# A table of offsets to a planner's priorities, and new planned durations, in a one-core attention and MLP kernel

## The chip, the cores and the metric

The kernel runs on one core of a Trainium2 chip. The metric is the device time of one execution in microseconds (us); lower is better.

## What is computed

Four sequences of 768 tokens with 8 heads of 64 pass through causal attention. Some heads ("retrieval" heads, by a flag that is read at run time) see all earlier keys; the others see the first 4 keys and a window of 64. The result, 3072 tokens by 512, goes through an MLP with `h - tanh(h)` between its two matrices.

```python
scores = scale * np.matmul(q, k.transpose(0, 1, 3, 2))
...
mask = np.where(retr[0, :, 0, 0, None, None], full_mask, stream_mask)
...
a = np.exp(scores)
a = a / (np.sum(a, axis=-1, keepdims=True) + 1e-09)
return np.matmul(a, v).astype(np.float32)
...
h = x @ w_in            # 512 -> 2048
g = h - np.tanh(h)
return (g @ w_out).astype(np.float32)   # 2048 -> 512
```

## The kernel before

The tokens are cut into 12 tiles of 256 (`TT`), three to a sequence. A tile passes through these stages, each of which has a letter in the text:

- **Load.** Tiles 0, 1 and 2 are loaded in heads as given (`load_first`, `load_cast`). From tile 3 on, q, k and v are loaded in FP32 by `load_raw` (L643), and POOL's `gather` (L688 for q and k, L724 for v) casts them and puts the heads in the order of their rank, retrieval heads first. The ranks are worked out on DVE in a chain of small operations (`by_rank`, the last is `perm_i`, L1019) and read into registers of POOL and DVE by a TENSOR_LOAD (L1068).
- **Turn.** q and k are transposed into the tile `QK`: by PE and a copy for tiles 0 to 2 (`st_T`: L1097, copies L1078 and L1080), by a DMA transpose from the queue of SP after that (`turn`, L607).
- **S.** `st_S` (L1220) makes scores in two banks of PSUM, ACT takes exp into `pt` or `ptn` (L1233), DVE multiplies by a mask (L1249, L1255, L1274, L1284). For tiles 0 and 1 PE adds the mask instead (L1179, L1182, L1198).
- **A.** `st_A` (L1313) multiplies by v (`v1`, and `vf` for keys further back), DVE divides (L1333, then L1360 or L1345).
- **X.** The result is transposed into `xT`: by PE for tiles 0 and 1, by a DMA transpose from SP's queue (`st_X_tile`, L1377) from tile 2 on.
- **H.** `H_unit` (L1437) multiplies xT by a quarter of `w_in` (tiles `win0` to `win3`); ACT takes tanh (L1449), DVE subtracts into `gt` (L1456; `gu` for tile 2).
- **O.** `O_group` (L1495) multiplies by `w_out`; ACT evicts (L1469) into one of three `ot` buffers, and SP stores (L1481). From tile 7 on the second product is done in seven smaller products (`piece`, L1619) with sums on DVE (L1586) and folds (L1673, L1654, L1684, stores L1704).
- PE runs 128-wide products of ones (L1938, "fills") in the gaps that the plan sees before 18 us.

Nothing is issued as it is written. Each call to `op` gives the planner one step with an engine, a planned duration in ns, what it reads and writes, and a priority, which is its index. `Plan.run` plays the whole program with these durations, and of the steps that could start at an engine's next free moment it takes the one of lowest priority. The order that comes out is written into the program; the chip runs each engine's list in that order, and an engine whose next step isn't ready waits even when a later step could run. The plan also picks the PSUM bank and the `ot` buffer of each step.

Of the kernel before, what the change touches and what calls it, by code (L numbers as in the profile page):

```python
# [11 lines left out]
XS = 4096.0  # L12
TT = 256
NB = TT // 128


class Plan:
# [11 lines left out]
    GRAB = 350  # L29
    RESULT = {"PE": 200, "ACT": 0, "DVE": 0, "POOL": 0, "SP": 0}  # L30

    def __init__(self, bufs):
        self.bufs = bufs
# [12 lines left out]
    def op(self, eng, ns, fn, r=(), w=(), dma=None, prio=None, port=False):  # L46
        i = len(self.ops)
        deps = set()
        for k in r:
            if k in self.writer:  # L50
                deps.add(self.writer[k])
            if k[0] in self.PSUM:
                deps.update(j for j in self.readers.get(k, ()) if self.ops[j][0] != eng)
            self.readers.setdefault(k, []).append(i)
        for k in w:
            if k in self.writer:
                deps.add(self.writer[k])
# [12 lines left out]
        return i  # L70

    def visit(self, waiting):
# [185 lines left out]
def kernel(  # L258
# [110 lines left out]
    TQ = 8  # L369
# [35 lines left out]

    def program(first):

        P = Plan(bufs)
        op = P.op
        rot = {}  # L410

# [113 lines left out]
        def load_v(t):  # L525

            b, g = divmod(t, NG)
            for i in range(NB):
                blk = g * NB + i
                dma(  # L530
                    "POOL", 900,
                    lambda i=i, blk=blk: nc.gpsimd.dma_start(
                        out=v1s[b]()[:, blk, :, 0:D],
                        in_=v[b, :, blk * 128 : blk * 128 + 128, :].rearrange("h p d -> p h d"),
                    ),
                    128 * H, 15.5, w=[("v1", b, blk, x) for x in range(2)],
                    lag=(1100, 1450) if t == 0 else WL,
                )
# [77 lines left out]
        def load_raw(t, behind=None, ring="SP"):  # L616
# [21 lines left out]
            for i in range(NB):  # L638
                s0 = g * TT + i * 128
                for x, src in enumerate((q, k, v)):  # L640
                    dma(
                        ring, {"SP": 600, "POOL": 900}[ring],
                        lambda i=i, x=x, src=src, s0=s0: engs[ring].dma_start(  # L643
                            out=r5()[:, i, x, :, :] if x < 2 else rv()[:, i, :, :],
                            in_=src[b, :, s0 : s0 + 128, :].rearrange("h p d -> p h d"),
                        ),
                        128 * H, 18.0, r=[("held", 4)] if t > 4 else [], paced=ring == "SP",
                        lag=RL if ring == "SP" else (1100, 1500),
                        w=[("rawqk", iq, x, i)] if x < 2 else [("rawv", iv, i)],
                    )  # L650

        def load_w_in(j):
            dma(
                "POOL", 780,
                lambda: nc.gpsimd.dma_start(
                    out=w_in_t[j][:],
                    in_=moe_w_in[:, j * 512 : (j + 1) * 512].rearrange("(cb p) f -> p cb f", p=128),
                ),
                512, 78.0, w=[("win", j)], lag=WL,
            )  # L660

        def load_w_out(half, part):
            c0, f0 = half * DM // 2, part * NFB // 2
            dma(
                "POOL", 900,
                lambda: nc.gpsimd.dma_start(
                    out=w_out_t[:, f0 : f0 + NFB // 2, c0 : c0 + DM // 2],
                    in_=moe_w_out[f0 * 128 : (f0 + NFB // 2) * 128, c0 : c0 + DM // 2].rearrange(
                        "(fb p) m -> p fb m", p=128
                    ),  # L670
                ),
                1024, 43.0, w=[("wout", half, part)], lag=WL,
            )


        def gather(t):
# [7 lines left out]
            for s_ in range(H):  # L684

                def qk(s_=s_):
# [33 lines left out]
            for s_ in range(H):  # L720

                def vv(s_=s_):
# [4 lines left out]
                    )  # L727

                op(
                    "POOL", 325, vv, r=["regsPOOL"] + [("rawv", iv, i) for i in range(NB)],  # L730
                    w=[("v1", b, g * NB + i, RANK[s_] // NGEN) for i in range(NB)],
                )

# [62 lines left out]
        def rank_constants():  # L796
            AT = [("t16", t16s[0][1], 0, 0)]
            op(
                "POOL", 300,
                lambda: nc.gpsimd.affine_select(  # L800
                    out=upto[:], in_=ones[:, 0 : H * H].rearrange("p (a c) -> p a c", a=H),
                    compare_op=ALU.is_ge, fill=0.0, base=0, pattern=[[1, H], [-1, H]],
# [9 lines left out]
        def constants():  # L812
# [6 lines left out]
            select(A4[:, 2, :], ones[:], 0.5, window_i - 1, -1, 1, "A4")  # L819
            select(sinks[:], ones[:], 0.5, n_sink_i - 1, 0, -1, "sinks")  # L820
            op(
                "DVE", 220,
                lambda: nc.vector.tensor_max(out=A4[:, 0, :], in0=A4[:, 2, :], in1=sinks[:]),
                r=["A4", "sinks"], w=["A40"],
            )
            select(A4[:, 2, :], A4[:, 2, :], 0.0, 0, 1, -1, "A4")
            select(A4[:, 3, :], ones[:], 0.5, -(128 - window_i + 1), -1, 1, "A43")
            op(
                "DVE", 220,
                lambda: nc.vector.tensor_max(out=A4[:, 1, :], in0=A4[:, 3, :], in1=sinks[:]),  # L830
                r=["A43", "sinks"], w=["A41"],
            )
# [2 lines left out]
            for o, n, a, b in (  # L835
# [2 lines left out]
            ):  # L838
                if a:
                    op(  # L840
                        "DVE", 130,
                        lambda o=o, n=n, a=a, b=b: nc.vector.tensor_scalar(
                            out=o, in0=n, scalar1=a, scalar2=b, op0=ALU.is_lt, op1=ALU.mult
                        ),
# [74 lines left out]
        def by_head(hp):  # L919
            for h in (2 * hp, 2 * hp + 1):  # L920
                if NE[h] == "A":
# [7 lines left out]
                    )  # L929
                    continue  # L930
                op(
                    "DVE", 130,
                    lambda h=h: nc.vector.tensor_scalar(
                        out=per_head[:, h, :], in0=ident16[:], scalar1=coef[:, h : h + 1],
                        scalar2=None, op0=ALU.mult,
# [4 lines left out]
        def masks(hp):  # L940
            for h in (2 * hp, 2 * hp + 1):
                if MK[h] == "A":
# [8 lines left out]
                    continue  # L951
                e = "POOL" if MK[h] == "P" else "DVE"
                op(
                    e, {"POOL": 600, "DVE": 320}[e],
                    lambda h=h, e=e: engs[e].tensor_scalar(
                        out=m4[:, h, :], in0=A4[:].rearrange("p a c -> p (a c)"),
                        scalar1=thr[:, h : h + 1], scalar2=-30000.0, op0=ALU.is_lt,
# [284 lines left out]
        def mask(n, b, g, hp, near, pt, pk):  # L1242
            if near:
# [219 lines left out]
        def store(t, ts, po, key, c0, c1, eng, ring):  # L1463
# [3 lines left out]
            def evac():  # L1467
# [9 lines left out]

            op(eng, 110 + 0.95 * (c1 - c0), evac, r=[key], w=[("ot", io), ("od",) + key])
            dma(
                ring, 420,  # L1480
                lambda: engs[ring].dma_start(out=out[t0 : t0 + 128, c0:c1], in_=ot()[:, c0:c1]),  # L1481
                128, (c1 - c0) * 0.18, r=[("ot", io)], lag=(500, 800),
            )
# [47 lines left out]
        def combine(k, h, fn, a, b, w=lambda: ()):  # L1531
            cs = slice(h * NC // TQ, (h + 1) * NC // TQ)
            op(
                "DVE", 90 + 860 * 2 // TQ,
                lambda: getattr(nc.vector, fn)(
                    out=T_(k)[:, cs, :], in0=a()[:, cs, :], in1=b()[:, cs, :]
                ),
# [567 lines left out]
```

## Time and profile before

| | us |
|---|---|
| three runs | 227.23, 228.61, 227.23; median 227.23 |
| profiled execution, first to last instruction (span) | 225.6 |
| median over the span: what lies around it | 1.6 |
| PE busy, of the span | 216.9 |
| PE weight loads / DVE / ACT / POOL busy | 169.1 / 172.2 / 143.5 / 112.2 |

The profiled execution has no time of its own beside its span in what was recorded, so the 1.6 us are taken from the median of the timed runs. The page's line of DMA shares has 9 tenths or more, with few exceptions, through the first 22 of 40 slices. A row of the timeline gives the start, the length, the engine (PEld is PE's weight load, SPq the queue of SP, on which DMAs are issued), the line, the operation, what it writes and reads, and in brackets how long the engine had been idle before and what ended that. A row of windows gives a stretch, its length, each engine's busy time (and its instructions), the granted clock, the DMA share and GB/s.

### The profile page before, as it was taken

What the parts mean: (1) busy time and instruction counts of PE and PEld (TensorE: products, weight loads), DVE (VectorE), ACT (ScalarE), POOL (GpSimd) and SP (SyncE); (2) the same over time, 40 slices, a digit from 0 to 9 for tenths busy, and PEclk for the clock granted to TensorE, in tenths of its full rate; (3) what the DMA queues carried; (4) which work ended last, traced back from release to release, by engine and by line L of the source; (5) the groups of instructions that cost most, each with busy time, mean ns of one, the idle gap of its engine ahead of it and who ended that gap; (6) DMA issues with size and microseconds to landing.
All of it is one profiled execution on the core that took longest, in us unless ns stands there. A gap on an engine that the chain in (4) does not pass through costs nothing.

```text
span 225.6 us, 6514 instructions
## 1 busy us (share of the span) xinstructions
PE 216.9 (96%) x2443; PEld 169.1 (75%) x2443; DVE 172.2 (76%) x443; ACT 143.5 (64%) x225; POOL 112.2 (50%) x243
## 2 busy tenths in 40 slices
PE   7799999999999999999999999999999999999991
PEld 6467798788886866776676677676898888988881
DVE  6977988696775966576997654778999689787792
ACT  4879859965467777664676677486567757345310
POOL 8999342892935639593917809283032021031140
PEclk9999999999999999999999999999999999999997
DMA  6999999999999999999995999954401402202023
GB/s 177 180 191 205 197 197 218 198 194 219 222 182 239 174 253 197 240 198 233 239 241 124 209 214 212 240 97 93 96 3 68 77 0 94 48 3 93 0 96 102
DMA packets 104133, 35.33 MB, mean 157 GB/s; under 512 B 90658, under 2 KB 102434, under 8 KB 104098
## 3 DMA queue, kind: packets, MB, share of 16 engines
q1 hardware_dynamic: 86128, 26.75, 58.9%
q0 software_dynamic: 17152, 7.60, 25.9%
q10 hardware_dynamic: 818, 0.52, 0.8%
q8 instruction: 20, 0.33, 0.6%
q14 instruction: 15, 0.12, 0.2%
HBM read 27.26 MB, written 6.29 MB: 149 GB/s over the span
## 4 chain that ended last, share of the span: by engine, by line
PE 82%; ACT 3%; DVE 1%; issue 1%; ACTq 0%
PE banks L1437 33%; PE banks L1495 22%; PE banks L1619 14%; PE banks L1220 7%; PE banks L1313 6%; ACT pt L1233 1%; ACT th L1449 1%; PE banks L1097 0%; DVE QK L1080 0%; ACT ot L1469 0%; DVE gt L1456 0%; DVE pt L1274 0%; DVE ot L1673 0%; DVE x L1360 0%; ACT xT L1078 0%
## 5 line engine op out<-in xcount | busy, mean ns | idle before, releaser
L1437 PE MATMUL banks<-xT,win 128*128 128x256 f16 x768 | 96.5, 273 | 0.3 <-ACT ot L1469 0.3
L1437 PEld LDWEIGHTS <-win 128*128 128x128 f16 x768 | 72.6, 98 | 15.2 <-DMA xT<-x16t 0.4
L1449 ACT ACTIVATE th<-banks 128x512 f32<-128x512 f32 x96 | 56.9, 603 | 38.7 <-PE banks L1437 34.9
L1456 DVE SCALAR_TENSOR_TENSOR gt<-th,banks 128x512 f16<-128x512 f32 x88 | 59.1, 677 | 15.5 <-ACT th L1449 14.8
L1233 ACT ACTIVATE pt<-banks 128x768 f16<-128x768 f32 (+1 forms) x60 | 52.8, 920 | 10.9 <-PE banks L1220 10.5
L1495 PE MATMUL banks<-wout,gt 128*128 128x256 f16 (+1 forms) x256 | 49.3, 326 | 0.3 <-ACT ot L1469 0.3
L688 POOL CAST t<-rawqk 128x256 f16 x72 | 29.1, 453 | 29.3 <-DMA rawqk<-in_k_dram 27.4
L1684 POOL TENSOR_TENSOR ot<-gu,ot 128x256 f32<-128x256 f32 x8 | 6.8, 856 | 51.8 <-ACT gu L1654 43.0
L1495 PEld LDWEIGHTS <-gt 128*128 128x128 f16 x256 | 23.2, 98 | 11.3 <-issue 1.6
L1345 DVE TENSOR_TENSOR x16t<-banks,rinv 128x128 f32 (+1 forms) x80 | 22.6, 284 | 1.0 <-DVE x16t L1345 0.2
L724 POOL CAST v<-rawv 128x128 f16 x72 | 22.2, 360 | 0.0
L1220 PE MATMUL banks<-QK 64*128 64x128 f16 (+1 forms) x364 | 21.0, 238 | 0.7 <-ACT QK L1078 0.7
L1233 ACT ACTIVATE ptn<-banks 128x1024 f16<-128x1024 f32 (+1 forms) x18 | 17.1, 952 | 4.6 <-PE banks L1220 2.4
L1220 PEld LDWEIGHTS <-QK 64*128 64x128 f16 x364 | 12.6, 94 | 8.5 <-issue 6.4
L1313 PEld LDWEIGHTS <-pt 128*128 128x128 f16 x420 | 16.0, 97 | 2.7 <-issue 1.5
L1619 PEld LDWEIGHTS <-m 128*128 128x128 f16 x160 | 15.4, 98 | 1.9 <-issue 0.2
L1284 DVE TENSOR_TENSOR pt<-pt,m4r 128x1024 f16<-128x1024 f16 (+1 forms) x18 | 12.4, 690 | 5.5 <-ACT pt L1233 5.3
L1313 PE MATMUL banks<-v,pt 128*128 128x65 f16 x220 | 16.2, 193 | 0.3 <-DVE xT L1080 0.3
L1255 DVE TENSOR_TENSOR ptn<-ptn,mS 128x1024 f16<-128x1024 f16 x12 | 9.2, 763 | 8.3 <-ACT ptn L1233 8.3
L1333 DVE RECIPROCAL rinv<-banks 128x4 f32<-128x4 f32 x48 | 8.5, 178 | 8.0 <-PE banks L1313 7.4
L1313 PE MATMUL banks<-vf,pt 128*128 128x65 f16 x200 | 13.0, 193 | 0.2 <-DVE gt L1456 0.2
L1469 ACT ACTIVATE ot<-banks 128x512 f32<-128x512 f32 (+1 forms) x18 | 9.2, 512 | 5.7 <-PE banks L1495 3.4
(120 smaller groups left out, 267.7 us busy)
## 6 DMA issues: line engine op xcount, KB each, us to landing
rawqk<-in_q_dram SPq DMA_DIRECT2D x18, 256.0 KB, 3.9
out_dram<-ot SPq DMA_DIRECT2D x18, 256.0 KB, 2.5
rawqk<-in_k_dram SPq DMA_DIRECT2D x17, 256.0 KB, 4.3
rawv<-in_v_dram SPq DMA_DIRECT2D x16, 256.0 KB, 4.6
win<-in_moe_w_in_dram POOLq DMA_DIRECT2D x4, 512.0 KB, 11.0
wout<-in_moe_w_out_dram POOLq DMA_DIRECT2D x4, 512.0 KB, 13.4
out_dram<-ot SPq DMA_DIRECT2D x10, 128.0 KB, 3.6
v<-in_v_dram POOLq DMA_DIRECT2D x6, 128.0 KB, 8.3
```

The source lines that it names most:

```text
L688: nc.gpsimd.tensor_copy(out=c5()[:, :, :, s_ : s_ + 1, :], in_=r5()[:, :, :, at, :])
L724: nc.gpsimd.tensor_copy(out=v1s[b]()[:, g * NB : g * NB + NB, RANK[s_] : RANK[s_] + 1, 0:D], in_=rv()[:, :, at, :],)
L1220: nc.tensor.matmul(out=sc()[:, hh, o : o + nb * 128], lhsT=lhsT, rhs=QK[p_, hp, q_0 : q_0 + nb * 128], start=not added, stop=not added or ...
L1233: lambda pt=pt, sc=sc, gi=gi, wid=wid: nc.scalar.activation(out=pt()[:, :, 512 * gi : 512 * gi + wid], in_=sc()[:, :, 0:wid], func=AF.Exp, ...
L1284: nc.vector.tensor_mul(out=pv, in0=pv, in1=m)
L1313: nc.tensor.matmul(out=av()[:, i, hh, :], lhsT=pt()[:, hh, co : co + 128], rhs=vv, start=(jb == first_jb), stop=(jb == qb),)
L1345: nc.vector.tensor_mul(out=xt()[:, :, at, :], in0=av()[:, :, hh : hh + 1, 0:D], in1=rinv()[:, :, hh : hh + 1].unsqueeze(3).to_broadcast([1 ...
L1437: nc.tensor.matmul(out=ph()[:, j, :], lhsT=w_in_t[fb // 4][:, cb, f0 : f0 + 128], rhs=x, start=(cb == 0), stop=(cb == HP - 1),)
L1449: lambda: nc.scalar.activation(out=th()[:], in_=ph()[:], func=AF.Tanh, scale=1.0 / XS),
L1456: lambda: nc.vector.scalar_tensor_tensor(out=gt()[:, u * FU : (u + 1) * FU, :], in0=th()[:], scalar=-XS, in1=ph()[:], op0=ALU.mult, op1=AL ...
L1495: nc.tensor.matmul(out=po()[:, c0:c1], lhsT=gt()[:, f, ts * 128 : ts * 128 + 128], rhs=w_out_t[:, f, c0:c1], start=(f == 0), stop=(f == NF ...
L1619: nc.tensor.matmul(out=po()[:, at : at + CM], lhsT=lhs(c), rhs=rhs(c), start=c == 0, stop=c == NC - 1,)
```

## The change

The same steps are given to the planner. Two things differ. First, some planned durations: the DMA issues (for instance 420 to 540 ns for a store, 600 to 620 for a raw load from SP), POOL's casts (450 to 404, 325 to 298), the masks (600 and 840 to 565 and 700), scores (160 + 0.44 per column to 190 + 0.427), and a few at the start. Second, a table `NUDGE` with some 1500 entries adds a number to the priority of the step of that index. Of the 1581 steps other than fills, none is added or taken away. The fills, whose number follows from the gaps that the plan sees, go from 54 products to 49.

```diff
+NUDGE = {
+    0: -535, 1: -798.5, 2: 2.9, 4: 63.5, 5: 16.8, 6: 64.8, 7: 250.1, 8: -93.7, 9: 40.5, 10: 81.9, 11: 197.6, 12: -24.3,
...
+}
...
-        self.ops.append((eng, ns, fn, deps, dma, i if prio is None else prio, port))
+        prio = (i if prio is None else prio) + self.nudge.get(i, 0)
+        self.ops.append((eng, ns, fn, deps, dma, prio, port))
...
-        P = Plan(bufs)
+        P = Plan(bufs, NUDGE if first else {})
...
-                        ring, {"SP": 600, "POOL": 900}[ring],
+                        ring, {"SP": 620, "POOL": 935}[ring],
...
-                    "POOL", 450, qk,
+                    "POOL", 404, qk,
...
-            todo, reads, keys, ns = [], [], [], 160
+            todo, reads, keys, ns = [], [], [], 190
...
-                ns += o * 0.44
+                ns += o * 0.427
...
-                op("DVE", 600 if g == 0 else 840, fn, r=pk + ["mS"], w=pk, port=True)
+                op("DVE", 565 if g == 0 else 700, fn, r=pk + ["mS"], w=pk, port=True)
...
-                ring, 420,
+                ring, 540,
                 lambda: engs[ring].dma_start(out=out[t0 : t0 + 128, c0:c1], in_=ot()[:, c0:c1]),
```

Line numbers of the changed kernel are 131 higher than before from the class `Plan` on, so L607 of before is L738 of the change.

The first place is DVE near the program's start. `t2` holds the per-head diagonals, `m4` the masks of tiles 0 and 1, and the copies into `QK` finish the turn of tile 0. Before:

```order
L933 TENSOR_SCALAR t2_151<-ident16_123,coef_132 128x128 x4
L955 TENSOR_SCALAR m4_128<-A4_124,thr_127 128x512
L933 TENSOR_SCALAR t2_151<-ident16_123,coef_132 128x128 x4
L955 TENSOR_SCALAR m4_128<-A4_124,thr_127 128x512 x2
L1080 CAST t16_0_215<-rawqk_0_158 128x2x256
L955 TENSOR_SCALAR m4_128<-A4_124,thr_127 128x512 x2
L1080 COPY QK_0_273<-banks_118 128x2x128 x6
```

And in the change:

```order
L1064 TENSOR_SCALAR t2_151<-ident16_123,coef_132 128x128 x5
L1211 CAST t16_0_218<-rawqk_0_158 128x2x256
L1064 TENSOR_SCALAR t2_151<-ident16_123,coef_132 128x128 x2
L1086 TENSOR_SCALAR m4_128<-A4_124,thr_127 128x512
L1211 COPY QK_0_268<-banks_118 128x2x128
L1064 TENSOR_SCALAR t2_151<-ident16_123,coef_132 128x128
L1211 COPY QK_0_268<-banks_118 128x2x128
L1086 TENSOR_SCALAR m4_128<-A4_124,thr_127 128x512 x2
L1211 COPY QK_0_268<-banks_118 128x2x128 x4
```

Four of the five masks and one diagonal now stand behind the first copy into `QK`.

The second place is POOL, which issues the loads of weights, of v (`v1`) and of tile 2 (`t16p_1`), and then those of tile 3 (`rawqk_1`). Before, from the second part of w_out on:

```order
L666 DMA wout_150<-in_moe_w_out_dram 128x8x256
L789 AFFINE_SELECT mS_137<-ones_121 64x128
L778 TENSOR_TENSOR vf_0_361<-v1_0_155,rflag_126 128x520
L566 DMA t16p_1_427<-in_q_dram 128x8x128
L566 DMA t16p_1_427<-in_k_dram 128x8x128
L532 DMA v1_0_155<-in_v_dram 128x8x64
L778 TENSOR_TENSOR vf_0_361<-v1_0_155,rflag_126 128x520 x2
L532 DMA v1_0_155<-in_v_dram 128x8x64
L643 DMA rawqk_1_558<-in_q_dram 128x8x64
L1068 TENSOR_LOAD perm_i_144
L643 DMA rawqk_1_558<-in_k_dram 128x8x64
```

The same stretch in the change:

```order
L663 DMA v1_0_155<-in_v_dram 128x8x64
L909 TENSOR_TENSOR vf_0_358<-v1_0_155,rflag_126 128x520
L797 DMA wout_150<-in_moe_w_out_dram 128x8x256
L931 AFFINE_SELECT upto_140<-ones_121 128x64
L920 AFFINE_SELECT mS_137<-ones_121 64x128 x2
L697 DMA t16p_1_454<-in_q_dram 128x8x128
L697 DMA t16p_1_454<-in_k_dram 128x8x128
L909 TENSOR_TENSOR vf_0_358<-v1_0_155,rflag_126 128x520
L663 DMA v1_0_155<-in_v_dram 128x8x64
L774 DMA rawqk_1_533<-in_k_dram 128x8x64
L909 TENSOR_TENSOR vf_0_358<-v1_0_155,rflag_126 128x520
L774 DMA rawqk_1_533<-in_q_dram 128x8x64
```

One load of v has moved from behind the loads of tile 2 to a place ahead of the second part of w_out, and the TENSOR_LOAD of the ranks, which stood between the loads of tile 3, now stands behind all of them and behind the last two parts of w_out. On DVE `perm_i`, which it reads, was made between evictions of tile 0's `gt`; in the change it stands behind all evictions of that tile and four of tile 1, and behind the copy into `QK` that ends the turn of tile 2's second pair of heads. Of the weights, which stand ahead of this stretch, `win2` and `win3` are now loaded before `win0`, and `win1` after the first part of w_out; PE's H steps follow that order.

The third place is the queue of SP from the first half of tile 3's turn to the transpose that makes `xT` of tile 2. `rawqk_2` and `rawv_1` are the loads of tile 4, `ot_1` to `ot_4` the first outputs. Before:

```order
L607 DMA_TRANSPOSE QK_1_965<-t16_3_904 128x8x128
L643 DMA rawqk_2_980<-in_q_dram 128x8x64
L643 DMA rawqk_2_980<-in_k_dram 128x8x64
L643 DMA rawv_1_982<-in_v_dram 128x8x64
L607 DMA_TRANSPOSE QK_1_965<-t16_3_904 128x8x128
L1481 DMA out_0_dram<-ot_1_985 128x256
L1481 DMA out_0_dram<-ot_2_1100 128x256
L643 DMA rawqk_2_980<-in_q_dram 128x8x64
L643 DMA rawqk_2_980<-in_k_dram 128x8x64
L1481 DMA out_0_dram<-ot_3_1145 128x256
L643 DMA rawv_1_982<-in_v_dram 128x8x64
L1481 DMA out_0_dram<-ot_4_1186 128x256
```

And in the change; the next row in each of the two is the DMA_TRANSPOSE of `xT_2`:

```order
L738 DMA_TRANSPOSE QK_1_957<-t16_3_888 128x8x128
L774 DMA rawqk_2_949<-in_q_dram 128x8x64
L774 DMA rawqk_2_949<-in_k_dram 128x8x64
L774 DMA rawv_1_951<-in_v_dram 128x8x64
L738 DMA_TRANSPOSE QK_1_957<-t16_3_888 128x8x128
L1612 DMA out_0_dram<-ot_1_969 128x256
L774 DMA rawqk_2_949<-in_q_dram 128x8x64
L1612 DMA out_0_dram<-ot_3_1096 128x256
L774 DMA rawqk_2_949<-in_k_dram 128x8x64
L1612 DMA out_0_dram<-ot_2_1112 128x256
L774 DMA rawv_1_951<-in_v_dram 128x8x64
L1612 DMA out_0_dram<-ot_4_1174 128x256
```

The same twelve issues stand ahead of that transpose; the stores and the loads alternate more evenly, and the store of `ot_3` comes before that of `ot_2`.

On PE, the set of steps ahead of the first H step of tile 2 is the same before and in the change, and so is the set ahead of the first S step of tile 4; two O steps (four products, each 256 wide) that stood ahead of the first S step of tile 3 now follow it.

More of the change, by code (lines that the diff above doesn't have):

```diff
@@ L530, in load_v @@
                 dma(
-                    "POOL", 900,
+                    "POOL", 1130 if t == 0 and i == 0 else 960,
                     lambda i=i, blk=blk: nc.gpsimd.dma_start(
@@ L653, in load_w_in @@
             dma(
-                "POOL", 780,
+                "POOL", 825,
                 lambda: nc.gpsimd.dma_start(
@@ L664, in load_w_out @@
             dma(
-                "POOL", 900,
+                "POOL", 935,
                 lambda: nc.gpsimd.dma_start(
@@ L729, in gather @@
                 op(
-                    "POOL", 325, vv, r=["regsPOOL"] + [("rawv", iv, i) for i in range(NB)],
+                    "POOL", 298, vv, r=["regsPOOL"] + [("rawv", iv, i) for i in range(NB)],
                     w=[("v1", b, g * NB + i, RANK[s_] // NGEN) for i in range(NB)],
@@ L798, in rank_constants @@
             op(
-                "POOL", 300,
+                "POOL", 520,
                 lambda: nc.gpsimd.affine_select(
@@ L821, in constants @@
             op(
-                "DVE", 220,
+                "DVE", 290,
                 lambda: nc.vector.tensor_max(out=A4[:, 0, :], in0=A4[:, 2, :], in1=sinks[:]),
@@ L828, in constants @@
             op(
-                "DVE", 220,
+                "DVE", 290,
                 lambda: nc.vector.tensor_max(out=A4[:, 1, :], in0=A4[:, 3, :], in1=sinks[:]),
@@ L840, in constants @@
                     op(
-                        "DVE", 130,
+                        "DVE", 330,
                         lambda o=o, n=n, a=a, b=b: nc.vector.tensor_scalar(
@@ L931, in by_head @@
                 op(
-                    "DVE", 130,
+                    "DVE", 248,
                     lambda h=h: nc.vector.tensor_scalar(
@@ L953, in masks @@
                 op(
-                    e, {"POOL": 600, "DVE": 320}[e],
+                    e, {"POOL": 600, "DVE": 345}[e],
                     lambda h=h, e=e: engs[e].tensor_scalar(
@@ L1533, in combine @@
             op(
-                "DVE", 90 + 860 * 2 // TQ,
+                "DVE", 90 + 800 * 2 // TQ,
                 lambda: getattr(nc.vector, fn)(
```

4 lines of the change are left out of this document (2 added, 2 removed), and 125 rows, old and new, of the table NUDGE.

## Prediction

> **What bounds the kernel now.** I read the page's busy times and chain first, then windows of PE, then what PE waited for, and last the queue of SP.
>
> ```profile
> span 225.6 us, 6514 instructions
> PE 216.9 (96%) x2443; PEld 169.1 (75%) x2443; DVE 172.2 (76%) x443; ACT 143.5 (64%) x225; POOL 112.2 (50%) x243
> PE 82%; ACT 3%; DVE 1%; issue 1%; ACTq 0%
> ```
>
> PE is the bound, and a new order of the same steps can only take away PE's pauses. The windows say where they are; the second number is the stretch, the third PE's busy time.
>
> ```profile
> 17.20:54.20 37.00, 36.48 (x479) 29.97 (x478) 30.40 (x83) 28.62 (x47) 22.34 (x37) 1.00 1.31 204
> 54.20:60.50 6.30, 6.03 (x83) 5.17 (x82) 4.41 (x15) 4.22 (x8) 4.30 (x12) 1.00 1.04 207
> 60.50:68.10 7.60, 7.58 (x68) 6.44 (x70) 5.31 (x9) 4.57 (x9) 3.97 (x12) 1.00 1.19 201
> 200.00:221.10 21.10, 21.06 (x193) 18.62 (x191) 17.15 (x34) 7.14 (x13) 4.67 (x6) 1.00 0.17 58
> ```
>
> From 17.2 to 60.5 PE pauses for 0.52 + 0.27 = 0.79 us; after 60.5 the two windows shown leave 0.02 + 0.04 = 0.06 us in 28.7 us, which for the 160.6 us up to 221.1 would be 0.3. A busy row hides short pauses, though: a matmul's row is longer than its spacing.
>
> ```profile
> L1437 PE MATMUL banks<-xT,win 128*128 128x256 f16 x768 | 96.5, 273 | 0.3 <-ACT ot L1469 0.3
> 210.58 1.75 PE banks L1437 x16
> 212.33 8.75 PE banks L1619 x80
> ```
>
> Sixteen H matmuls take 1.75 us, 0.109 each, where one row says 0.273, so each pause may be longer by 0.16 than it looks. I therefore take the pauses as once to twice what the windows say: 0.8 to 1.6 us between 17.2 and 60.5, 0.3 to 0.6 after that. That is all there is to win past the start, about 2 us.
>
> The 75% of PEld could be read otherwise. The Trainium skill, in "Perfetto Trace Analysis", section "Identifying the Most-Contended Engine", calls PE's matmul share a poor measure of the distance to the roof and names the share of weight loads instead; by it 225.6 - 169.1 = 56 us would be open to a better order. The trace doesn't bear that out as room for an order: in 200 to 221.1 us the loads fill 18.62 of 21.10, and yet the last 80 matmuls follow each other at 8.75 / 80 = 0.109 us like the H steps above, without a pause. Nothing below rests on it.
>
> Two of PE's pauses matter more than their length, since what ends them isn't PE's order.
>
> ```profile
> 54.13 0.33 PEld L1220 LDWEIGHTS <-QK 64*128 64x128 f16 x8 [0.21 <-issue]
> 54.27 0.29 POOL L713 COPY kc<-QK 128x128 f16<-128x128 f16 x1 [2.78 <-DMA QK<-t]
> 60.52 0.33 PEld L1437 LDWEIGHTS <-win 128*128 128x128 f16 x4 [0.42 <-DMA xT<-x16t]
> ```
>
> At 54.1 PE begins S of tile 3, and within 0.2 us POOL, which waited 2.78 us for the same DMA transpose of `QK`, is released: PE came just in time. At 60.52 H of tile 2 begins when `xT` lands, after 0.42 us of waiting. (The page names ACT's `ot` for the matmul there; the weight load's row names the DMA.) Both transposes come from SP's queue:
>
> ```profile
> 44.14 1.85 SPq L607 DMA_TRANSPOSE QK<-t  x1
> 46.26 0.39 SPq L643 DMA_DIRECT2D rawqk<-in_q_dram  x1
> 46.70 0.57 SPq L643 DMA_DIRECT2D rawqk<-in_k_dram  x1
> 47.33 0.87 SPq L643 DMA_DIRECT2D rawv<-in_v_dram  x1
> 48.24 2.26 SPq L607 DMA_TRANSPOSE QK<-t  x1
> 50.55 1.06 SPq L1481 DMA_DIRECT2D out_dram<-ot  x2
> ...
> 54.96 0.75 SPq L1481 DMA_DIRECT2D out_dram<-ot  x1
> 55.81 1.57 SPq L1377 DMA_TRANSPOSE xT<-x16t  x1
> ```
>
> Of the eight issues shown each begins within 0.3 us of the end of the one above it, and the five left out stand as closely: the queue hardly rests from 44.14 to 57.4. It begins when POOL has cast tile 3, and that begins when tile 3's load lands:
>
> ```profile
> 40.39 3.73 POOL L688 CAST t<-rawqk 128x256 f16 x8 [4.74 <-DMA rawqk<-in_k_dram]
> 54.44 0.38 ACT L1469 ACTIVATE ot<-banks 128x256 f32<-128x256 f32 x1 [2.31 <-DMA out_dram<-ot]
> 53.30 0.49 DVE L1345 TENSOR_TENSOR x16t<-banks,rinv 128x128 f16<-128x128 f32 x2
> ```
>
> 40.39 + 3.73 = 44.12. DVE had what `xT` is made of by 53.79, 2.0 us before its transpose was issued; ACT stood 2.31 us for an `ot` buffer whose store had gone out at 50.55, behind the transpose. So up to 60.5 us a **chain of loads, POOL and SP** sets the time, and PE with its pauses fits under it.
>
> **The change, part by part.** *Start.* DVE's first copies for tile 0:
>
> ```profile
> 6.54 0.73 DVE L955 TENSOR_SCALAR m<-A,thr 128x512 f16<-128x512 f16 x2
> 7.53 0.92 DVE L955 TENSOR_SCALAR m<-A,thr 128x512 f16<-128x512 f16 x2
> 8.37 2.09 DVE L1080 COPY QK<-banks 128x256 f16<-128x256 f16 x6
> 7.35 0.60 ACT L1078 CAST t<-rawqk 128x512 f16<-128x512 f32 x1
> 8.83 0.78 ACT L1078 COPY QK<-banks 128x256 f16<-128x256 f16 x2 [0.88 <-DVE QK L1080]
> 17.23 1.03 PE L1437 MATMUL banks<-xT,win 128*128 128x256 f16 x8
> ```
>
> Four masks now follow the copy. A pair takes 0.73 or 0.92, some 0.4 each, so DVE is free some 1.6 us earlier; PE's transposes and ACT's cast, which ends at 7.95, then hold it, and ACT's copy can start at 7.95, not 8.83: the first S is **0.7 to 0.9 us earlier**. The first H of 17.23 doesn't move, because ACT's last copy into `xT` now stands behind two exps and a copy; but the second S of tile 1, which came after two H steps, is done before it. I take 0.7 us of PE's work gained. Five fills fewer cost and bring nothing; they stand in waits.
>
> *Loads.* Their volume ahead of the last q and k of tile 3 is the same, and the windows above show 204 and 207 GB/s throughout. So I leave POOL's start on tile 3 at 40.4. `win0` now lands third, but PE asks for `win2` first. Tile 2's q and k lie one load of v later, which is 128 KB as written and twice that as read:
>
> ```profile
> v<-in_v_dram POOLq DMA_DIRECT2D x6, 128.0 KB, 8.3
> ```
>
> At 204 GB/s that is 0.6 or 1.3 us. PE has two O steps more (0.44 us) ahead of that turn, so between 0 and 0.9 us of new waiting near 34 us, 0.4 taken.
>
> *SP, 44 to 57 us.* The same twelve issues precede `xT` of tile 2. Between the two halves of tile 3's turn there are three loads, before and after. The store that ACT waits for is again the first behind the second half. So S of tile 3 stays at 54.1 and `xT` at 60.5: 0 us, with an uncertainty of a store or load moved, 0.4 to 0.9 by their rows, either way.
>
> *PE, 17 to 60 us.* Ahead of S of tile 3 PE now has two O steps fewer: 4 x 0.109 = 0.44 us. With the 0.7 of the start, less 0.4 near 34, and some of the 0.5 us of pauses gone, it arrives 0.7 to 1.3 us early, and waits to 54.1. From there to H of tile 2 its weight loads took from 54.13 to 60.10, where the idle 0.42 ahead of 60.52 began, 5.97 us; with 0.44 more it is at 54.13 + 6.41 = 60.5, exactly when `xT` lands. **All of the early gain is waited away**: 0 us at 60.5.
>
> *60.5 to 68 us.*
>
> ```profile
> 60.52 7.16 PE banks L1437 x64
> 67.69 0.43 PE banks L1495 x2
> 68.12 0.49 PE banks L1220 x10
> 67.78 0.29 POOL L713 COPY kc<-QK 128x128 f16<-128x128 f16 x1 [0.55 <-DMA QK<-t]
> ```
>
> H and one O step lead to S of tile 4 at 68.12, with the same steps ahead of it as before; its `QK` is there at 67.78 at the latest, when POOL's copy starts. Even if `xT` came earlier, only 0.3 us could be kept here unless SP's queue moved as a whole.
>
> *After that.* Tile 5's last q or k load is issued one transpose and one load earlier than before, so nothing there is later. Of the remaining pauses of 0.3 to 0.6 us I take 0.3 as gone. The products and the last fold are the same, and so is what follows the last matmul at 221.1.
>
> **Sum**, against the span of 225.6 us: 0 at 60.5, -0.3 after, 225.3. With the 1.6 us around it, **226.9 us**; the median of the runs shown is 227.23.
>
> **The rivals.** *The chain moves too.* The two transposes of tile 3 took 1.85 and 2.26 us to issue, where the shortest of that line take 1.23:
>
> ```profile
> L607 SPq DMA_TRANSPOSE QK<-t x18: 1232/1327/3033, 44.1 to 152.6; - x18
> ```
>
> If other neighbours bring both to 1.23, SP is 1.65 us earlier at `xT` and at tile 4's turn alike, and PE's 0.7 + 0.8 us can be kept: 226.9 - 1.5 = 225.4, at most 224.5 with all pauses gone. For it: the alternation of stores and loads. Against it: those around the two transposes are the same. Chance 0.20.
>
> *The ranks come late* (slower). POOL can't cast tile 3 before it has the ranks:
>
> ```profile
> 24.47 0.16 DVE L1019 TENSOR_SCALAR perm_i<-pos_a 128x8 int32<-128x8 f32 x1
> 26.34 0.89 POOL L643 DMA_DIRECT2D rawqk<-in_k_dram  x1 [3.62 <-DVE rinv L1333]
> 35.52 0.45 DVE L1080 COPY QK<-banks 128x256 f16<-128x256 f16 x1 [0.49 <-ACT QK L1078]
> ```
>
> Before, `perm_i` was there at 24.63 and POOL went on at 26.34, 1.7 us for the reading. Now `perm_i` follows the copy of 35.52, which may come up to 1.3 later with tile 2's load, and four small operations (0.2 each, as its own row says): 36.8 to 38.1. With 1.7 POOL is ready at 38.5 to 39.8, against 40.39. It decides from the moment that `perm_i` is later than 38.7; beyond it each us delays tile 3's turn, its S, and the steps behind it. A tile 2 that turns 4 us later than I think puts it 3 us over, which PE's cover doesn't reach, since S waits for `QK` itself: 226.9 + 3 = 230. Chance 0.15.
>
> *Nothing at all*: the new durations concern a plan and not the chip, and neither the pauses after 60.5 nor the two waits at 54.1 and 60.5 us change: 227.2. It lies in my forecast's own range, 226.2 to 227.8, which holds 0.65 with it.
>
> **How the numbers follow.** Forecast 0.65, the chain moving 0.20, ranks 0.15. The range reaches down to 224.9, between the 225.4 and the floor of 224.5, and up to 229.3, most of the way to the 230: it leaves out some 0.13 of the second rival's 0.15 and a third of the first's 0.20. Over 1% faster is below 225.0, over 1% slower above 229.5; 1% is about what a measurement of this kernel tells from no change. Faster: a good half of the first rival, 0.13; slower: most of the second, 0.12; same 0.75.
>
> **What would show it.** Right: ACT's first copy into `QK` at about 8.0 and not 8.83 us; S of tile 3 at 54 after a visible wait of PE; H of tile 2 at 60.5; 160.5 us from there to the last matmul. Wrong: if H of tile 2 starts before 60, the chain moved, and SP's transposes at 44 to 50 us will be short or early; if POOL's first cast of tile 3 starts after 40.7, the ranks or the loads were late; if more than 160.8 us follow H of tile 2, the new order has stalls of its own in the part where PE is alone.

## The result, and the profile after

The change is slower: 228.87 us (median of 12 runs, 228.24 to 229.75) against 227.49 for the kernel before on the same chip, a ratio of 1.0055 with a 95% interval from 1.0035 to 1.0075. Forecast were 226.9, 0.14% faster. Medians, ratios and intervals, here and below, are of the fast runs: one run of e4 and three of g1 were slow and are left out. The profiled executions differ by nearly as much, 226.8 against 225.6 us of span, so they can be used to look for the loss. The page of the change, its first lines and its chain:

```profile
span 226.8 us, 6489 instructions
PE 216.5 (95%) x2438; PEld 169.2 (75%) x2438; DVE 172.6 (76%) x443; ACT 143.7 (63%) x225; POOL 111.4 (49%) x243
PE 87%; DVE 4%; ACT 4%; issue 2%; DMA 1%; POOL 0%; DVEq 0%; POOLq 0%; ACTq 0%
```

PE's work is what it was (216.9 before). Of the chain, DVE now has 4% where it had 1%, and a DMA has 1%. Three of the prediction's windows, for the change (start and end, the stretch, then PE's busy time):

```profile
54.20:60.50 6.30, 6.30 (x86) 5.50 (x86) 4.48 (x14) 3.76 (x6) 3.08 (x8) 1.00 0.86 193
60.50:68.10 7.60, 7.60 (x73) 6.46 (x73) 6.25 (x13) 4.92 (x9) 4.93 (x15) 1.00 1.04 202
200.00:221.10 21.10, 20.84 (x192) 18.49 (x189) 16.77 (x36) 7.49 (x15) 5.44 (x7) 1.00 0.15 52
```

From 54.2 to 68.1 PE doesn't pause at all, where it was idle for 0.29 us before. In the last stretch it is the other way: 0.26 us, 0.04 before. The timeline of the change shows the two places that the prediction had set at 54.1 and 60.5, and the first S:

```profile
7.56 0.76 ACT L1209 COPY QK<-banks 128x256 f16<-128x256 f16 x2
8.26 0.50 PE L1351 MATMUL banks<-QK 64*128 64x256 f16 x8
...
52.62 0.40 POOL L844 COPY kc<-QK 128x128 f16<-128x128 f16 x1 [1.17 <-DMA QK<-t]
54.23 0.33 PEld L1351 LDWEIGHTS <-QK 64*128 64x128 f16 x10 [0.21 <-issue]
60.53 1.55 PEld L1568 LDWEIGHTS <-win 128*128 128x128 f16 x15
```

S of tile 3 begins at 54.23 (54.13 before) and H of tile 2 at 60.53 (60.52). In these two traces the change has neither gained nor lost up to here. Other executions vary, though: seven traces with the change's order in this part begin H of tile 2 (first product) between 60.26 and 61.49, the middle one at 60.68, and two of the kernel before at 60.52 and 60.29. A loss of some tenths of a us up to here can't be excluded. What follows is the end. First the tail of the kernel before, in its timeline (the last two stores of SP and the two of ACT share a row each):

```profile
220.02 1.04 PE L1619 MATMUL banks<-wout,m 128*128 128x256 f16 x8
219.43 1.65 SPq L1704 DMA_DIRECT2D out_dram<-ot  x2
221.07 1.21 ACTq L1704 DMA_DIRECT2D out_dram<-ot  x2
```

And of the change:

```profile
219.35 0.42 DVE L1804 SCALAR_TENSOR_TENSOR ot<-banks,gu 128x256 f32<-128x256 f32 x1 [1.06 <-DMA out_dram<-ot]
219.81 0.42 DVE L1804 SCALAR_TENSOR_TENSOR gu<-banks,ot 128x256 f32<-128x256 f32 x1
...
219.43 0.60 PE L1750 MATMUL banks<-wout,gt 128*128 128x256 f16 x4
220.29 1.03 PE L1750 MATMUL banks<-wout,m 128*128 128x256 f16 x8 [0.26 <-DVE gu L1804]
...
221.12 1.94 SPq L1835 DMA_DIRECT2D out_dram<-ot  x2
220.78 1.39 ACTq L1835 DMA_DIRECT2D out_dram<-ot  x2
```

Two things are to be seen. DVE stands 1.06 us until a store has landed and its `ot` buffer is free; the fold after it comes late, and PE, whose last product needs the bank that this fold empties, waits. The four products from 219.43 take 4 x 0.109 = 0.44 us, so the next could begin at 219.87; it begins at 220.29, and 0.42 us are lost (its row shows 0.26, for the reason given in the prediction). And of the last four stores the first goes out at 220.78; before it was 219.43. The last matmul ends at 220.29 + 1.03 = 221.32 and the span, to the hundredth, is 226.77, so 5.45 us follow it; before, it was 225.62 - 221.06 = 4.56. In both traces the last store is issued about 0.5 us after the last matmul, and the end comes 1.8 to 1.9 us after the last landing. What differs is when the stores land.

**The sum of the difference:** 0.04 at H of tile 2 (first products at 60.56 and 60.52), -0.20 in the work from there, +0.42 for PE's wait, +0.89 behind the last matmul: 1.15 us, which is 226.77 - 225.62.

How it comes about: the columns of the last tile that the kernel calls E lie in the buffer `ot_27`. Two folds write to it (steps 1592 and 1596), but only the one that is written first in the program, 1592, names the buffer to the planner:

```python
def own(t, x):
    ...
    return [("ot", unit(t, x)[1])] if ("ot", t, x) not in outs else []
```

The table lets DVE run 1596 four places ahead of 1592, and moves the second half of 1592's product behind two others on PE. The plan gives `ot_27` a buffer when 1592 runs; 1596, which is already through by then in the plan, gets it too and waits on the chip for a store of which the plan knows nothing. With 1592 its store (1593) goes late as well. In the order before, 1596 also runs first, but by one place only, and no wait is seen at it.

### The profile page after: what moved, and what is told of

It reads as the page before. It is cut to its first block, busy times and chain, and to the rows that moved or that the text cites. A ratio compares the mean times of both kernels' runs of the same rounds, so it can differ in the third digit from the quotient of the medians.

```text
span 226.8 us, 6489 instructions
## 1 busy us (share of the span) xinstructions
PE 216.5 (95%) x2438; PEld 169.2 (75%) x2438; DVE 172.6 (76%) x443; ACT 143.7 (63%) x225; POOL 111.4 (49%) x243
## 4 chain that ended last, share of the span: by engine, by line
PE 87%; DVE 4%; ACT 4%; issue 2%; DMA 1%; POOL 0%; DVEq 0%; POOLq 0%; ACTq 0%
PE banks L1568 37%; PE banks L1626 22%; PE banks L1750 10%; PE banks L1351 8%; PE banks L1444 7%; DVE ot L1804 1%; ACT pt L1364 1%; PE banks L2069 1%; ACT th L1580 1%; DMA out_dram<-ot 1%; ACT m L1076 1%; DVE QK L1211 1%; PE banks L1228 1%; ACT t L1209 1%; DVE m L1717 1%
## 5 line engine op out<-in xcount | busy, mean ns | idle before, releaser
L1626 PE MATMUL banks<-wout,gt 128*128 128x256 f16 (+1 forms) x256 | 48.4, 326 | 0.0
L819 POOL CAST t<-rawqk 128x256 f16 x72 | 30.5, 468 | 18.8 <-DMA rawqk<-in_k_dram 11.9
L1626 PEld LDWEIGHTS <-gt 128*128 128x128 f16 x256 | 23.4, 98 | 11.7 <-issue 1.4
L855 POOL CAST v<-rawv 128x128 f16 x72 | 20.2, 327 | 6.2 <-DMA rawv<-in_v_dram 6.2
L1444 PEld LDWEIGHTS <-pt 128*128 128x128 f16 x420 | 16.5, 97 | 4.5 <-issue 1.9
L1444 PE MATMUL banks<-v,pt 128*128 128x65 f16 x220 | 16.7, 193 | 1.4 <-DVE x L1491 1.4
L1415 DVE TENSOR_TENSOR pt<-pt,m4r 128x1024 f16<-128x1024 f16 (+1 forms) x18 | 13.0, 721 | 4.6 <-ACT pt L1364 3.7
L1815 POOL TENSOR_TENSOR gu<-gu 128x256 f32<-128x256 f32 x4 | 3.3, 831 | 22.0 <-ACT gu L1785 22.0
## 6 DMA issues: line engine op xcount, KB each, us to landing
v<-in_v_dram POOLq DMA_DIRECT2D x6, 128.0 KB, 11.7
```

The lines of the kernel that those rows point to most:

```text
L819: nc.gpsimd.tensor_copy(out=c5()[:, :, :, s_ : s_ + 1, :], in_=r5()[:, :, :, at, :])
L855: nc.gpsimd.tensor_copy(out=v1s[b]()[:, g * NB : g * NB + NB, RANK[s_] : RANK[s_] + 1, 0:D], in_=rv()[:, :, at, :],)
L1415: nc.vector.tensor_mul(out=pv, in0=pv, in1=m)
L1444: nc.tensor.matmul(out=av()[:, i, hh, :], lhsT=pt()[:, hh, co : co + 128], rhs=vv, start=(jb == first_jb), stop=(jb == qb),)
L1626: nc.tensor.matmul(out=po()[:, c0:c1], lhsT=gt()[:, f, ts * 128 : ts * 128 + 128], rhs=w_out_t[:, f, c0:c1], start=(f == 0), stop=(f == NF ...
```

## The experiments

Times are medians, ratios those to the kernel before on the same chip in the same comparison. The kernels of a group ran on one chip. The kernel before had 227.49 us in the first timing and 227.42 in group 1, but 228.38 and 228.32 in groups 2 and 3, so kernels are best compared within a group. The ratios are as recorded; they aren't the quotients of the medians.

| kernel | us | ratio | 95% interval |
|---|---|---|---|
| group 1: buffer alone (e1) | 228.25 | 1.0036 | 1.0018 to 1.0053 |
| buffer, three steps moved (e2) | 228.27 | 1.0038 | 1.0019 to 1.0057 |
| swap on POOL (e3) | 228.64 | 1.0050 | 1.0035 to 1.0065 |
| e2 with the swap (e4) | 227.83 | 1.0012 | 0.9995 to 1.0029 |
| group 2: tail as before, with the swap (f1) | 227.53 | 0.9975 | 0.9953 to 0.9998 |
| tail as before (f2) | 227.77 | 0.9967 | 0.9944 to 0.9990 |
| kernel before, one store later (f3) | 228.47 | 0.9996 | 0.9970 to 1.0021 |
| durations alone (g1) | 230.48 | 1.0088 | 1.0057 to 1.0118 |
| group 3: the change (h1) | 228.98 | 1.0021 | 0.9995 to 1.0048 |
| buffer alone (h2) | 228.52 | 1.0018 | 0.9994 to 1.0043 |
| tail as before (h3) | 227.70 | 0.9978 | 0.9955 to 1.0000 |
| table alone (h4) | 236.10 | 1.0349 | 1.0307 to 1.0391 |

Steps were moved in the finished order, one by one, so that nothing else shifts; a new number in the table would have changed the whole plan behind it.

**e1 and h2: a buffer of its own.** The edit puts `ot_27` into memory that is free by then:

```diff
+                    if first and (tag, i) == ("ot", 27):
+                        e = pools["ptn"].tile(*shape["ptn"], tag="ptn0", name="ot_27")
+                        box.append(e[:].bitcast(FP32).rearrange("p a b -> p (a b)"))
+                        return box[0]
```

> The changed kernel, same order of all steps, but the last `ot` buffer (ot_27) lies in memory of its own, so that DVE's fold at 219.35 us needn't wait for the store that landed at 219.23. Theory A, the tail (that wait, and the late stores behind it, are the loss of 226.8 - 225.6 us): the fold starts at 218.75, PE's pause of 0.42 us ahead of its last eight products goes, the last matmul ends at 220.9 instead of 221.32, and the span falls by 0.4 to 226.4; against before 1.0035. Rival B, the loss is made at the start (DVE's copy that lasts 1.78 us at 11.72) and the tail only hangs behind it: PE's pause goes, but the span stays within 0.1 of 226.8. Rival D, the stores that are issued within 1 us of each other set the end by themselves: the last matmul ends 0.4 earlier and the end stays at 226.8.

> The changed kernel with the last `ot` buffer in memory of its own. Theory A: PE's pause of 0.42 us ahead of its last eight products is all that goes: 0.4 to 0.5 us less than the change itself. Rival: nothing, if the stores behind it set the end.

Timeline and page of h2:

```profile
span 226.2 us, 6489 instructions
218.65 0.43 DVE L1808 SCALAR_TENSOR_TENSOR ot<-banks,gu 128x256 f32<-128x256 f32 x1 [0.54 <-PE banks L1754]
...
219.25 0.60 PE L1754 MATMUL banks<-wout,gt 128*128 128x256 f16 x4
219.69 1.04 PE L1754 MATMUL banks<-wout,m 128*128 128x256 f16 x8
```

DVE now waits for PE and not for a store, and PE's last eight follow after 0.44 us: the wait is gone. What comes after the last matmul has not changed: the span of 226.17 less 220.72, where it ends, is 5.45 us. In e1 the last matmul ends at 220.90, 0.42 us earlier than in the change. The times agree but don't settle it: e1's ratio is 0.0019 lower than the change's own, which is 0.43 us of 227.4, and h2 took 0.46 us less than the change (h1) beside it by the medians, but only 0.07 by the ratios (1.0018 and 1.0021). The intervals overlap, so it is the traces that carry this.

**e2: the store 1.3 us earlier.** Beside the buffer, three moves (a is put ahead of b):

```diff
+        for a, b in ((1591, 1601), (1592, 1605), (1593, 1605)) if self.nudge else ():
+            order.remove(a)
+            order.insert(order.index(b), a)
```

> As the run with the buffer of its own, and three steps of the tail moved: the second half of the product for the E columns 0 (PE), its fold (DVE) and its store (SP) stand ahead of the last two products, so that a store goes out at 220.0 us and not at 221.56. Theory A: the last matmul ends at 220.9, the last store is issued at 221.4, the end comes 4.5 us after the last matmul as before (5.45 in the change): span 225.4 to 225.5, ratio to before 0.999. Rival D (what follows the last matmul doesn't depend on which store goes when): span 226.3 to 226.4. Rival B: not under 226.4.

A miss: 228.27, the same as e1. Its traced execution had 5.79 us behind the last matmul, that of e4 with the same tail 5.11. In e4 the four stores went out from 219.53 on, 0.8 us ahead of the last matmul's end, with the others 0.38, 0.71 and 1.26 us behind the first: they still overlap.

**f2 and h3: the tail as before.** Instead of these moves, PE's products stand in the order of the kernel before, and the fold and the store of columns E 0 ahead of the others:

```diff
+        for a, b in ((1586, 1598), (1588, 1598), (1591, 1598), (1594, 1598), (1595, 1598),
+                     (1592, 1596), (1593, 1604)) if self.nudge else ():
```

> As the run above without the swap on POOL: only the tail is put back. Theory A: the last matmul ends at 220.9, the end 4.6 us later: span 225.5, ratio to before 1.000: the tail explains the whole loss of the change. Rival: ratio 1.0036 as with the buffer alone, and the rest of the loss is at the start.

> The changed kernel itself, to stand beside the next two on one chip: the two tail runs so far were timed against a kernel before that was 0.9 us slower and wider (227.15 to 229.81) than in the other comparisons. Expected from its first timing: 228.9 us, or ratio 1.003 to 1.0055.

> The buffer, and the tail in the order of the kernel before. Theory A: the first of the four last stores goes out 1.6 us and not 0.1 us before the last matmul ends, the end comes 4.6 to 4.8 us after it instead of 5.4: 1.0 to 1.3 us less than the change itself, and level with before, 0.998 to 1.001. Rival: the good ratio of 0.9967 was the other chip's slow kernel before, and this is no more than 0.5 us under the change.

The change itself showed the same tail again in its second trace (the 1.06 us wait of DVE for the store to the hundredth). h3 took 227.70 against 228.98 beside it: **1.28 us less** by the medians, 0.98 by the ratios (0.0043 of 228.3). The traces promise 0.42 of it for the wait. For the rest, every trace that has one of these tails can be set side by side:

| the last stores | us from the last matmul to the end |
|---|---|
| as in the change (change, h1, e3, e1, h2) | 5.45, 5.77, 5.24, 5.54, 5.45 |
| the first of them 0.8 us ahead of the last matmul's end (e2, e4) | 5.79, 5.11 |
| kernel before, one store later (f3, below) | 5.12 |
| the first 2.25 us ahead (f1, f2, h3) | 4.86, 4.79, 5.02 |
| kernel before, the first 1.63 us ahead | 4.56 |

Where a store leaves 1.6 us or more ahead of the last matmul's end, 4.56 to 5.02 us follow it; elsewhere it is 5.11 to 5.79, and the two groups don't overlap. One order alone spreads over 0.5 us and more, so the 0.89 of the first two traces is not known better than that. In all twelve the last store leaves 0.5 us after the last matmul and the end comes 1.8 to 1.9 us after the last landing. Page and timeline of h3:

```profile
span 226.0 us, 6489 instructions
219.98 1.04 PE L1757 MATMUL banks<-wout,m 128*128 128x256 f16 x8
...
218.77 2.54 SPq L1842 DMA_DIRECT2D out_dram<-ot  x2
220.64 2.14 ACTq L1842 DMA_DIRECT2D out_dram<-ot  x2
```

The first store leaves at 218.77, 2.25 us ahead of the last matmul's end, and 5.02 us follow that end. With the tail put back the rest of the change is level with the kernel before or a little better (0.9978, 0.9967). In these two groups, though, the kernel before was itself 0.9 us slower than at first; beside the 227.4 to 227.5 of the other two comparisons, 227.70 and 227.77 would be 0.2 to 0.4 us more. So the tail explains the loss as far as these comparisons can tell, and a few tenths elsewhere stay open. (It isn't wholly the tail of the kernel before: DVE keeps the change's order of the two folds 1605 and 1603, so that ACT's first store leaves ahead of SP's.)

**f3: the kernel before with the change's order of SP's last two stores.** The reverse test: one move on SP, nothing else.

```diff
+        for a, b in ((1593, 1610),) if n > 1500 else ():
```

> The kernel before with one edit: on SP the store of the last tile's E columns 0 stands behind that of its F columns 0 and not ahead of it, so that it is issued at 221.1 us and not at 219.43; nothing else moves. Theory A: four stores go out within 1 us, and the end comes 5.1 to 5.4 us after the last matmul instead of 4.56: span 226.2 to 226.4, ratio 1.003. Rival (the order of stores is of no weight): 225.6, ratio 1.000.

```profile
span 227.2 us, 6513 instructions
221.08 1.04 PE L1622 MATMUL banks<-wout,m 128*128 128x256 f16 x8
...
221.79 1.32 SPq L1707 DMA_DIRECT2D out_dram<-ot  x2
222.12 0.99 ACTq L1707 DMA_DIRECT2D out_dram<-ot  x2
```

The four stores leave within 0.8 us, and 5.12 us follow the last matmul, 0.56 more than 4.56: the trace is as expected. The time is not: 1.003 was expected, and the interval around 0.9996 ends at 1.0021, which is 0.48 us. By the time it is the rival that came true, by which the order of the stores is of no weight. So the reverse test doesn't confirm a loss of 0.56 us; 4.56 is one trace, and where the usual tail is nearer to the 4.8 to 5.0 of f1, f2 and h3 the move costs less. This execution's last matmul was later too, for reasons at 72 and 82 us:

```profile
72.28 0.92 PE L1440 MATMUL banks<-xT,win 128*128 128x256 f16 x7 [0.35 <-DMA xT<-x16t]
82.09 0.56 PE L1223 MATMUL banks<-QK 64*128 64x256 f16 x10 [0.73 <-DMA QK<-t]
```

Up to SP's last stores this order is that of the kernel before, and here PE waits twice for SP's transposes where the first trace shows no wait. In all ten traces with the change's order from there (the change twice and eight of its variants), H of tile 4 follows H of tile 3 by 15.37 to 15.39 us; here it was 16.12, and 15.32 in the first trace of the kernel before. One trace isn't a proof, but it fits the wider spread of the kernel before on that chip (227.15 to 229.81).

**e3, e4 and f1: the stall at the start.** In the change DVE's copy of the first half of a load took 0.28 us and that of the second 1.78, while POOL had no gap; PE waited for what DVE does next:

```profile
9.75 0.28 DVE L1211 COPY t<-t16p 128x512 f16<-128x512 f16 x1
...
11.72 1.78 DVE L1211 COPY t<-t16p 128x512 f16<-128x512 f16 x1
...
11.45 0.81 POOL L786 DMA_DIRECT2D win<-in_moe_w_in_dram  x1
12.22 1.12 POOL L909 TENSOR_TENSOR vf<-v,rflag 128x520 f16<-128x520 f16 x1
...
14.10 0.35 PE L1444 MATMUL banks<-v,pt 128*128 128x65 f16 x6 [1.39 <-DVE x L1491]
```

The copy began ahead of the row at 12.22 and ended at 13.50, 0.16 after that row. The edit swaps two steps of POOL:

```diff
+        for a, b in ((76, 130),) if self.nudge else ():
```

> The changed kernel with one swap on POOL: the DMA issue for a part of v1 stands ahead of the first multiplication for vf instead of behind it. Theory P: DVE's copy into t at 11.72 lasts 1.78 us because POOL works without a gap from 11.80 on and DVE can't get at the memory before that ends; with the swap the copy gets in at 12.26 and ends at 12.55, PE goes on at 13.1 and not at 14.1. Rival: the copy waits for its data; then it ends at 13.5 as now. What follows, by the theory of the prediction (the chain of SP sets the time at 60.5): S of tile 3 at 53.2, H of tile 2 at 60.0 to 60.1 when xT lands, and only 0.5 of the 1.0 us stays: span 226.3, ratio 1.003. By the rival that PE alone sets the time: H of tile 2 at 59.6, span 225.8, ratio 1.001.

> Both edits, the tail's (buffer of its own and the three steps moved) and the swap on POOL. Theory A with the chain: -1.3 and -0.5, span 225.0, ratio to before 0.997. With PE alone: 224.5, 0.995. If the swap brings nothing: 225.4.

> The changed kernel with the last `ot` buffer in memory of its own, the swap on POOL, and the order of the tail as in the kernel before: products of the last tile in the order 4, 2, 6, 5, 7, 3 on PE, and the fold and the store of the E columns 0 ahead of the others. Theory A (buffer wait and late first store make the loss of the tail): the store goes out 1.6 us before the last matmul ends, the end comes 4.6 us after it instead of 5.4; the last matmul ends at 220.3 as in the run with both edits, so the span is 224.9, ratio to before 0.998. Rival (what follows the last matmul doesn't hang on that store): 225.4, ratio 1.001.

In e3's traced execution the load itself landed late, so that the copy waited for its data and took 0.29 us; e4 (0.27 us) and f1 show the swap undisturbed. The timeline of f1:

```profile
11.54 0.62 DVE L1218 COPY t<-t16p 128x512 f16<-128x512 f16 x1
...
12.99 0.36 PE L1451 MATMUL banks<-v,pt 128*128 128x65 f16 x6
...
53.52 0.34 PEld L1358 LDWEIGHTS <-QK 64*128 64x128 f16 x10 [0.21 <-issue]
56.20 0.24 PEld L1451 LDWEIGHTS <-ptn 128*128 128x128 f16 x6 [0.60 <-DVE ptn L1387]
60.30 1.76 PEld L1575 LDWEIGHTS <-win 128*128 128x128 f16 x17
```

The copy takes 0.62 us and PE goes on at 12.99, 1.11 us earlier. At S of tile 3 it is 0.71 earlier, then PE waits 0.60 for DVE, and at H of tile 2 it is 0.23. On the clock it is e3 against the change 0.0005, e4 against e2 0.0026, f1 against f2 -0.0008: between 0.6 us won and 0.2 lost. The gain at the start is seen in the traces; at the end nothing is left of it that these comparisons can tell.

**g1 and h4: each part alone.** The one has an empty table, `NUDGE = {}`, the other the table in the kernel before, with its old durations.

> One part of the change alone: the new planned durations, with an empty table. The planner's own end for this order lies 4.4 us after its end for the order before, so if the plan is to be believed the time is 2% longer: 231.5 us, ratio 1.019, and the table's work is to win this back. Rival: better durations alone make a better order: ratio 0.997, and what the change loses is the table's. Third: the plan's differences of such a size mean nothing on the chip: within 1%, 0.995 to 1.005.

> The other part of the change alone: the table, with the durations of before. The table was searched for the new durations; with the old ones the planner's own end lies 7.3 us later than for the kernel before. If the plan is to be believed 2 to 3% longer, 1.02 to 1.03; the new durations alone were 4.4 us later in the plan and 2.0 us by the median on the chip, so by that share 1.015. Rival: the table's order is good whatever the plan's durations: 0.998 to 1.005.

Both are slower, by 0.9% and 3.5%, or 2.1 and 7.8 us by the medians; the planner's own ends had been 4.4 and 7.3 us later. The new durations alone make a worse order, and with the table beside them 0.2 to 0.55% of the 0.9 are left (h1 and the first timing); with other durations the same numbers do more harm than good.

## Why the prediction was wrong, point by point

- **The step that failed** is this: "The products and the last fold are the same, and so is what follows the last matmul at 221.1." The last fold was the same, but not the order of those ahead of it, nor that of the last stores. The prediction went through the orders at the start and from 44 to 68 us, and not through the last rows of each queue, where 1596 and 1592 stand. This term was put at 0 us; the first two traces show 0.42 + 0.89 = 1.31, and putting the tail back brought 1.28 by the medians and 0.98 by the ratios. That 1.31 and 1.28 are so close is luck, since what follows the last matmul varies by half a us between executions.
- **S of tile 3 at 54.1 and H of tile 2 at 60.5:** right in time (54.23, 60.53), wrong in cause, and so right by luck. I said PE would come early and wait for SP. It didn't wait: the loss came at 11.7 to 14.1 us, where the copy behind the moved masks was held. SP's chain was meanwhile earlier itself: `QK` of tile 3 by 1.65 us by POOL's row (52.62 for 54.27), and `xT`, which landed at 60.0 and not 60.5 (its transpose was issued at 56.66, 3.3 us before; in the kernel before at 55.81, 4.7 us before). So the rival of the chain that moves, which I gave 0.20, was true in part, and PE was too late to use it. The floor that I named didn't hold PE in f1 either: its rows show no wait at 60.30, but 0.60 us for DVE at 56.20, and of the 1.1 us from the start 0.23 were left at H.
- **The start:** ACT's first copy came at 7.56, not "about 8.0"; the gain of 0.7 to 0.9 us at the first S was 1.07 (8.26 for 9.33). That four masks behind the copies could meet POOL's work I had not priced at all. And the first H, which by the prediction "doesn't move" from 17.23, came at 18.38; with the swap on POOL (f1, the second row) it was at 17.21:

```profile
18.38 1.38 PE L1568 MATMUL banks<-xT,win 128*128 128x256 f16 x11
17.21 1.05 PE L1575 MATMUL banks<-xT,win 128*128 128x256 f16 x8
```

- **60.5 us to the last matmul:** -0.3 forecast; -0.20 without the wait in the tail (160.34 us, as in six of the eight variants with this order, for 160.54 before). That part was right. With the wait it was 160.76, just under the 160.8 that was to show stalls of the order's own, so that sign stayed silent.
- **The ranks come late:** it didn't decide. The timeline of the change, POOL at 38 to 40 us:

```profile
38.62 0.32 POOL L600 MEMSET v<- 128x48 f16 x1 [3.50 <-DVE perm_i L1150]
40.22 3.73 POOL L819 CAST t<-rawqk 128x256 f16 x8 [1.28 <-DMA rawqk<-in_q_dram]
```

  POOL has the ranks by 38.62, inside the 38.5 to 39.8 that I had worked out, and then waits 1.28 us for its load, so the cover held.
- **The 1.6 us around the span** are too few: in each timed execution that has both numbers, time less span is 1.7 to 1.9 us. The 1.6 were a median less the span of one execution. This accounts for 0.1 to 0.3 of the 1.97 us by which the forecast was off.
- **The range** of 224.9 to 229.3 holds the measured 228.87, and "same" within 1% was the likeliest case; the sign was wrong, for a rival that wasn't on my list.

## What to carry to other kernels

When steps are reordered, read the last rows of every queue as closely as those of the bound engine: there nothing is behind them that could hide a late step. A planner must be told every writer of a buffer, not just the first in program order, or a new order will hit a wait that the plan doesn't have. A table of corrections belongs to the durations that it came with: each part of such a change can be worse alone than both together.

## What the runs showed of the hardware

**Stores that leave close together landed later, in most of these traces.** In the kernel before, the tile of the output buffers shows 2.2 to 2.3 us from issue to landing for the last four stores, of which the first left 1.3 us ahead; in the change, with all four within 1.1 us, 2.7 to 3.4; in f3, with all four within 0.8 us, 2.1 to 3.0:

```profile
DMA to landing us min/median/max: 2.2/2.3/2.3
DMA to landing us min/median/max: 2.7/3.1/3.4
DMA to landing us min/median/max: 2.1/2.5/3.0
```

It isn't a plain rule: in h3, where the first store had landed before the other three left, these took 2.7 to 2.9 us, more than in the kernel before, and with one order (e4 and e2) the first took 3.1 us in one execution and 3.8 in another. What makes a landing late stays open.

**DVE was held by two instructions of POOL in a row.** The copy that takes 0.28 us at 9.75 lasted 1.78 from 11.72 on, through the end of a DMA issue and the whole multiplication that followed. Three more traces show the same at this place, with the mask that stands ahead of the copy: 1.95 us in h1, 1.70 in e1, 1.66 in e2, each from within the DMA issue to 0.16 us after the multiplication. The Trainium skill, in "SBUF — State Buffer", section "Who interferes with whom", says of DVE instructions in a two-port mode that they share a pair of ports with POOL, that the first to issue has it for its whole instruction, and that the other fully blocks. The wait agrees, though no run here shows the mode of the copy; that the copy also stayed behind POOL's next instruction goes further than the rule, which speaks of one instruction. With a DMA issue behind it instead the copy got in after 0.62 us (f1), and in e4, where it began 0.04 us after the start of POOL's issue, it took 0.27.
